# Key and value loads of a cached-attention decode block: from SyncE's queue to GpSimd's, with a signal from ScalarE to TensorE

## The chip, the cores and the metric

The kernel runs on one core of one Trainium2 chip. The metric is device time in microseconds (us), the median of several runs. A core has TensorE (PE), VectorE (DVE), ScalarE (ACT), GpSimd (POOL) and SyncE (SP); transfers from the chip's memory run on the core's 16 DMA engines, and any of SyncE, ScalarE and GpSimd can issue them from its instruction stream.

## What is computed

One decode step of a transformer block for 2 sequences: attention with a cached K and V of 8192 positions and 32 heads of 128 elements, then a gated feed-forward, all in float32.

```
h  = x + attention(layernorm(x), k_cache, v_cache, wq, wo)      # q = x wq; softmax(q k / sqrt(128)) v; times wo
h2 = h + (silu(n w_gate) * (n w_up)) w_down,  n = layernorm(h)
x [2,1,512]   k_cache, v_cache [2,32,8192,128]   wq [512,4096]   wo [4096,512]
w_gate, w_up [512,1792]   w_down [1792,512]
```

K and V together are 537 MB, nearly all that is read.

## The kernel before

The work is cut into 32 units. A unit `i` is two heads of one sequence: one head lies on partitions 0 to 63, the other on 64 to 127, and each partition holds 128 positions of 128 elements, 64 KB. So one K load and one V load are 8.39 MB each. There are two buffers for K (`kslot`, unit `i` uses number `i % 2`) and one for V (`vslot`). The buffers are used again at the two ends: `vslot` first holds wq and last w_down, and the two K buffers hold wo, and the gate and up weights, once their K is used up.

The loads stand in one list, `loads`, in this order: wq; K 0 in four parts; then K 1, V 0, K 2, V 1, and so on to K 31, V 30; then wo in two parts; V 31 in four parts; the gate and up weights in four parts; w_down in five. Before, SyncE issues them all in that order (L578 to L581), and ahead of a load into a used buffer it waits until the buffer's last reader is done (`after`, `freed`). For K `i` that is VectorE's last reduction over K `i-2`; for V `i` it is TensorE's last value matmul of unit `i-1`; for V 0 the last matmul of the query projection; for wo it is K 30, for V 31 it is V 30, for the gate and up weights K 31, for w_down V 31.

A round of the loop at L403, unit `i`, puts on VectorE: multiply the first half of K `i` with the query (L412); the maximum over partitions for unit `i-1` (`biggest`, L365); reduce the first half (L421); multiply the second half; the reciprocal of the softmax sum of unit `i-1` (`recip`, L391); reduce the second half; the maximum of the scores (L429). Unit 0 is done in four quarters. ScalarE has per round, for unit `i-1`: copy the negated maximum (L372), two exponentials (L378), then `rdiag` (L393), which needs the reciprocal of L391, then the copy of the value product (`osb`, L398) and of the transposed result (L400). ScalarE works through its instructions in order.

TensorE's rounds are a counted loop (`pe_rounds`, L342): the maximum's transpose (L314), its broadcast (L316, L317), the softmax sums (L319), then a wait for V, then the 64 value matmuls (`pe_values`, L324), then four small matmuls per unit (L337) that scale and transpose. The wait for V is on semaphore `s_v`, which each load raises by 16 and which TensorE lowers by 16 each round. The last unit's values are taken in four parts behind the loop, as the parts of V 31 land (L473).

GpSimd sets up constants (L207 to L216, L263), does one small power operation in each of the two layer norms (L236), and nothing else. `g.steps` holds each engine's instructions in the order in which the program adds them; `wait` leaves a wait out where the engine has already waited for as much.

Of the kernel before, what the change touches and what calls it, by code (L numbers as in the profile page):

```python
# [9 lines left out]
P = 128  # L10
# [3 lines left out]
class Program:  # L14
# [16 lines left out]
    def wait(self, engine, *points):  # L31
        for s, value in points:
            if self.known[engine].get(s, 0) < value:
                self.known[engine][s] = value
                self.steps[engine].append(lambda e, s=s, v=value: e.wait_ge(s, v))

    def do(self, engine, fn, sem=None, by=1):

        if sem is None:
            self.steps[engine].append(fn)  # L40
            return None
        self.count[sem] += by
        self.steps[engine].append(lambda e: fn(e).then_inc(sem, by))
        return sem, self.count[sem]
# [8 lines left out]
def decode_block(nc, x, k_cache, v_cache, wq, wo, w_gate, w_up, w_down, out):  # L53
# [24 lines left out]
    def sbuf(name, *shape, align=32):  # L78
        return nc.alloc_sbuf_tensor(name, list(shape), F32, align_bytes=align).ap()
# [7 lines left out]
    vslot = sbuf("vslot", P, SLOT, align=512)  # L87
# [38 lines left out]
    g = Program(nc)  # L126
    wait, do = g.wait, g.do
# [2 lines left out]
    s_dve, s_act, s_pe, s_pool = (g.sem(n) for n in ("dve", "act", "pe", "pool"))  # L130
    s_dve_pe, s_act_pe, s_v = (g.sem(n) for n in ("dve_pe", "act_pe", "v"))
    s_k = [g.sem(f"k{n}") for n in range(2)]

    def alone(name):
        return g.sem(name)
# [3 lines left out]
    landed = {}  # L139
    freed = {}  # L140
    loads = []
# [5 lines left out]
    def load_kv(kind, i, parts=1):  # L147
        cache, t = (k_cache, kslot[i % 2]) if kind == "k" else (v_cache, vslot)
        n = SLOT // parts
        for c in range(parts):  # L150
            sem = alone(f"{kind}{i}_{c}") if parts > 1 else s_k[i % 2] if kind == "k" else s_v
            loads.append(((kind, i), c, t[:, c * n : (c + 1) * n], k_src(cache, i)[:, c * n : (c + 1) * n], sem))

    loads.append((("wq", 0), 0, vslot, wq.rearrange("(p c) m -> p (c m)", p=P), s_v))
    load_kv("k", 0, 4)
    for i in range(1, U):
        load_kv("k", i)
# [21 lines left out]
    for e, (c, n) in enumerate(WF):  # L179
        src, c0 = (w_gate, c) if c < DC else (w_up, c - DC)  # L180
# [18 lines left out]
    after = {("v", 0): ("wq", 0), ("wo", 0): ("k", U - 2), ("wf", 0): ("k", U - 1), ("wd", 0): ("v", U - 1)}  # L199
# [28 lines left out]
    def layernorm(src, ready):  # L228
        wait("vector", *ready)
        p = do("vector", lambda e: e.bn_stats(stats, src), s_dve)  # L230
        wait("vector", p)
        p = do("vector", lambda e: e.bn_aggr(mv, stats), s_dve)
        wait("vector", p)
        p = do("vector", lambda e: e.tensor_scalar(ve, mv[:, 1:2], EPS, None, op0=OP.add), s_dve)
        wait("gpsimd", p)
        p = do("gpsimd", lambda e: e.tensor_tensor(rstd, ve, mhalf, op=OP.pow), s_pool)  # L236
        wait("vector", p)
        p = do(
            "vector",
            lambda e: e.tensor_scalar(y, src, mv[:, 0:1], rstd, op0=OP.subtract, op1=OP.mult),  # L240
            s_dve,
        )
        normed = p
        wait("tensor", p, ident_done)
        for c in range(DC):
            p = do(
                "tensor",
                lambda e, c=c: e.transpose(yt[:, c, :], y.rearrange("b (p c) -> b c p", c=DC)[:, c, :], ident[:B, :B]),
                s_pe if c == DC - 1 else None,
            )  # L250
        return normed, p

    _, p = layernorm(xs, [(x_in, 16)])
# [14 lines left out]
    p = do("vector", lambda e: e.tensor_copy(xT, yt), s_dve)  # L268
# [10 lines left out]
    for n, (m, b) in enumerate((m, b) for m in range(0, MQ, 4) for b in range(B)):  # L279
# [3 lines left out]
        for c in range(DC):  # L283
            for k in range(2):
                p = do(
                    "tensor",
                    lambda e, ps=ps, c=c, k=k, m=m, b=b: e.matmul(  # L287
                        ps[HALF[k]],
                        xb[:, c * B + b, :],
                        wqv[:, c, k, m : m + 4, :],  # L290
                        start=(c == 0),
                        stop=(c == DC - 1),
                    ),
# [40 lines left out]
    def pe_outputs(e):  # L334
        e.wait_ge(s_act_pe, 2)
        for a in range(W):
            inst = e.matmul(  # L337
                ot_ps, osb[:, a * DH : (a + 1) * DH], rdiag[:, a::W], start=(a == 0), stop=(a == W - 1)
            )
        inst.then_inc(s_pe, 1)  # L340

    def pe_rounds(e):  # L342
        e.sem_inc(s_v, -16)
        with nc.Fori(0, U - 1, engines=[PE], head_slot={PE: 0}):
            pe_scores(e)
            e.wait_ge(s_v, 16)
            pe_values(e, 0, NW)
            pe_outputs(e)
            e.sem_inc(s_dve_pe, -2)
            e.sem_inc(s_act_pe, -2)  # L350
            e.sem_inc(s_v, -16)
        pe_scores(e)

    g.steps["tensor"].append(pe_rounds)
# [6 lines left out]
    def biggest(i):  # L361
        wait("vector", at(i, MROW))
        do(
            "vector",
            lambda e: e.tensor_reduce(gm, mrow.rearrange("p (k r) -> p k r", k=2), axis=AX.X, op=OP.max),  # L365
            s_dve_pe,
        )
# [21 lines left out]
    def recip(i):  # L389
        wait("vector", at(i, DEN))  # L390
        p = do("vector", lambda e: e.reciprocal(r, den), s_dve)  # L391
        wait("scalar", p)
        do("scalar", lambda e: e.activation(rdiag, diag, AF.Copy, scale=r))  # L393
# [9 lines left out]
    for i in range(U):  # L403
        m, b = divmod(i, B)
        parts = 4 if i == 0 else 2
        n = NJ // parts
        wait("vector", q_done[m // 4 * B + b])
        for c in range(parts):
            wait("vector", landed[("k", i), c if i == 0 else 0])
            kt = k_view(i, c * n, n)  # L410
            qb = qsb[:, b, m, :][:, None, :].to_broadcast([P, n, DH])
            mult = do("vector", lambda e, kt=kt, qb=qb: e.tensor_tensor(kt, kt, qb, op=OP.mult), s_dve)  # L412
            if i and c == 0:
                biggest(i - 1)
                softmax(i - 1)
            if i and c == 1:
                recip(i - 1)
            wait("vector", mult)
            p = do(
                "vector",  # L420
                lambda e, kt=kt, s=scores[i % 2][:, c * n : (c + 1) * n]: e.tensor_reduce(s, kt, axis=AX.X, op=OP.add),  # L421
                s_dve,
            )
        freed["k", i] = p
        if i:
            oT_done[i - 1] = outputs(i - 1)
            freed["v", i - 1] = at(i - 1, PV)
        wait("vector", p)
        do("vector", lambda e, s=scores[i % 2]: e.tensor_reduce(m1, s, axis=AX.X, op=OP.max), s_dve_pe)  # L429
    biggest(U - 1)  # L430
    softmax(U - 1)
    do("scalar", lambda e: e.activation(warm, mhalf[:1, :], AF.Sigmoid))
# [10 lines left out]
    for c in range(4):  # L443
        for q in range(4):
            p = do(
                "tensor",
                lambda e, c=c, q=q: e.matmul(
                    oq_ps[32 * q : 32 * q + 32, c], ident[:, c::4], oT[:, q:QH:4, :], start=True, stop=True
                ),
                s_pe if c == 3 and q == 3 else None,  # L450
            )
    wait("scalar", p)
    p = do("scalar", lambda e: e.activation(oq, oq_ps, AF.Copy), s_act)
# [3 lines left out]
    for n, (o, w) in enumerate(pairs):  # L457
        t = n % 4
        p = do(
            "tensor",  # L460
            lambda e, n=n, t=t, o=o, w=w: e.matmul(
                wide[0][32 * t : 32 * t + B, :], o, w, start=(n < 4), stop=(n >= len(pairs) - 4)
            ),
            s_pe if n == len(pairs) - 1 else None,
        )
    wait("scalar", p)
    p = do("scalar", lambda e: e.activation(osb, wide[0], AF.Copy), s_act)
# [56 lines left out]
    p = project_f(0, gate)  # L524

    wait("tensor", h1_done)
    for t in range(4):
# [8 lines left out]
    p = do("scalar", lambda e: e.activation(sg, gate, AF.Sigmoid), s_act)  # L536
    wait("vector", p)
    sg_done = do("vector", lambda e: e.tensor_mul(sg, gate, sg), s_dve)
    p = project_f(DC, up)
# [4 lines left out]
    p = do(  # L544
        "vector",
        lambda e: e.tensor_mul(
            gu.rearrange("p (c j) -> p j c", c=FB),
            up.rearrange("p (j c) -> p j c", c=FB),
            sg.rearrange("p (j c) -> p j c", c=FB),
        ),  # L550
        s_dve,
    )
    gT = rest[:, D + 2 * FQ : D + 3 * FQ]
    wait("vector", p)
    p = do("vector", lambda e: e.transpose(gT, gu), s_dve)
    wait("tensor", p)
    for c in range(FB):
# [3 lines left out]
        for t in range(4):  # L561
            p = do(
                "tensor",
                lambda e, c=c, t=t: e.matmul(  # L564
                    f_ps[32 * t : 32 * t + 32, :],
                    gT[:, c * 32 : (c + 1) * 32],
                    vslot[:, c * D + t * P : c * D + (t + 1) * P],
                    start=False,
                    stop=(c == FB - 1),
                ),  # L570
# [4 lines left out]
    res_done = do("vector", lambda e: e.tensor_copy(res, f_ps), s_dve)  # L575


    for item, e_, dst, src, sem in loads:  # L578
        if item in after:
            wait("sync", freed[after[item]])  # L580
        do("sync", lambda e, dst=dst, src=src: e.dma_start(dst, src), sem, 16)  # L581
    stored = []
    for b, engine in enumerate(("sync", "scalar")):
        wait(engine, res_done)
# [52 lines left out]
```

## Time and profile before

| | |
|---|---|
| time, median of 3 runs | 1310.69 us (1310.65 to 1310.78) |
| span of the profiled execution | 1309.4 us |
| VectorE busy | 1131.0 us (86%) |
| TensorE matmuls busy | 432.7 us (33%) |
| ScalarE busy | 80.3 us (6%) |
| read from memory | 564.66 MB, 431 GB/s over the span |
| K loads 1 to 31, issue to landing (median) | 42.4 us |
| V loads 0 to 30, issue to landing (median) | 29.3 us |

The span is the time from the first to the last instruction of the one execution that was profiled; the times of the runs also hold what lies around it. In the profile PE is TensorE's matmuls, PEld its weight loads, and "SPq" the stream in which SyncE issues transfers. A line of the timeline gives start, duration, engine, line of the code, operation, the tiles written and read, their shapes and the count; in brackets stands the idle time of the engine before it and what ended that. A row of the windows gives the stretch, the busy time of PE, PEld, DVE, ACT and POOL with their counts, TensorE's granted clock, the share of time in which the DMA engines were busy, and GB/s. A row of the waits gives total, times, longest. A row of the queues gives packets, MB, and the share of the 16 engines' span.

### The profile page before, as it was taken

What the parts mean: (1) busy time and instruction counts of PE and PEld (TensorE: products, weight loads), DVE (VectorE), ACT (ScalarE), POOL (GpSimd) and SP (SyncE); (2) the same over time, 40 slices, a digit from 0 to 9 for tenths busy, and PEclk for the clock granted to TensorE, in tenths of its full rate; (3) what the DMA queues carried; (4) which work ended last, traced back from release to release, by engine and by line L of the source; (5) the groups of instructions that cost most, each with busy time, mean ns of one, the idle gap of its engine ahead of it and who ended that gap; (6) DMA issues with size and microseconds to landing.
All of it is one profiled execution on the core that took longest, in us unless ns stands there. A gap on an engine that the chain in (4) does not pass through costs nothing.

```text
span 1309.4 us, 6768 instructions
## 1 busy us (share of the span) xinstructions
PE 432.7 (33%) x2980; PEld 135.3 (10%) x2980; DVE 1131.0 (86%) x248; ACT 80.3 (6%) x271; POOL 2.9 (0%) x13
## 2 busy tenths in 40 slices
PE   3633223333213333312333321333332133332175
PEld 1210001011001011100101100101110010110022
DVE  1999888889888889988888988888998888898841
ACT  0100000000000000000000000000000000000010
POOL 0000000000000000000000000000000000000000
PEclk9865566666556666656666655666655666665589
DMA  9999999999999999999999999999999999999998
GB/s 401 435 442 426 438 435 434 439 426 442 422 442 422 444 432 436 438 426 442 422 442 422 444 434 434 439 426 440 424 441 424 442 436 432 440 424 442 414 429 368
DMA packets 12990, 564.79 MB, mean 431 GB/s; under 512 B 1322, under 2 KB 1330, under 8 KB 2484
## 3 DMA queue, kind: packets, MB, share of 16 engines
q1 hardware_dynamic: 12968, 564.67, 99.7%
q8 instruction: 5, 0.08, 0.0%
q14 instruction: 5, 0.04, 0.0%
q10 hardware_dynamic: 12, 0.01, 0.0%
HBM read 564.66 MB, written 0.00 MB: 431 GB/s over the span
## 4 chain that ended last, share of the span: by engine, by line
DMA 75%; PE 24%; issue 0%; SPq 0%; DVE 0%
DMA vslot<-in_A_v_cache_dram 72%; PE opart L324 22%; PE wide L287 2%; DMA vslot<-in_A_wq_dram 2%; DMA vslot<-in_B_w_down_dram 2%; SPq L581 0%; PE bank L564 0%; DVE kslot L575 0%
## 5 line engine op out<-in xcount | busy, mean ns | idle before, releaser
L412 DVE TENSOR_TENSOR kslot<-kslot,qsb 128x8192 f32<-128x8192 f32 (+1 forms) x66 | 555.9, 8422 | 127.4 <-DMA kslot<-in_A_k_cache_dram 104.4
L421 DVE TENSOR_REDUCE s<-kslot 128x64 f32<-128x8192 f32 (+1 forms) x66 | 555.5, 8417 | 0.1
L324 PE MATMUL opart<-vslot,pz 128*8 128x512 f32 x2048 | 293.7, 736 | 253.7 <-DMA vslot<-in_A_v_cache_dram 253.7
L316 PE MATMUL bank<-gm,nscale 1*64 1x1 f32 x64 | 11.8, 251 | 361.7 <-DVE gm L365 361.7
L324 PEld LDWEIGHTS opart<-vslot,pz 128*8 128x8 f32 x2048 | 57.4, 103 | 463.0 <-DMA vslot<-in_A_v_cache_dram 257.9
L314 PE MATMUL bank<-ident,m 128*1 128x128 f32 x64 | 18.7, 395 | 163.3 <-DVE m L429 163.3
L316 PEld LDWEIGHTS bank<-gm,nscale 1*64 1x64 f32 x64 | 9.1, 199 | 377.7 <-DVE gm L365 377.7
L337 PE MATMUL bank<-rdiag,osb 128*128 128x2 f32 x256 | 33.7, 254 | 23.7 <-ACT osb L398 23.7
L393 ACT ACTIVATE rdiag<-diag,r 128x8 f32<-128x8 f32 x32 | 9.6, 301 | 484.6 <-DVE r L391 484.6
L372 ACT ACTIVATE nb<-bank 128x1 f32<-128x1 f32 x32 | 5.5, 171 | 550.2 <-PE bank L317 550.2
L337 PEld LDWEIGHTS bank<-rdiag,osb 128*128 128x128 f32 x256 | 31.0, 191 | 53.4 <-ACT osb L398 53.4
L287 PE MATMUL wide<-vslot,osb 128*64 128x512 f32 x128 | 29.6, 626 | 17.5 <-DMA vslot<-in_A_wq_dram 17.5
L319 PE MATMUL bank<-rs,sides 128*128 128x1 f32 x64 | 18.8, 363 | 41.5 <-ACT pz L378 41.5
L378 ACT ACTIVATE pz<-s,nb 64x128 f32<-64x128 f32 x64 | 25.5, 399 | 1.4
L398 ACT ACTIVATE osb<-opart 128x512 f32<-128x512 f32 x32 | 19.1, 597 | 76.6 <-PE opart L324 76.6
L230 DVE BATCH_NORM_STATS2 ln_stats<-attn 2x6 f32<-2x512 f32 x1 | 0.7, 687 | 25.2 <-PE attn L489 25.2
L319 PEld LDWEIGHTS bank<-rs,sides 128*128 128x128 f32 x64 | 16.1, 313 | 44.2 <-ACT pz L378 44.2
L314 PEld LDWEIGHTS bank<-ident,m 128*1 128x1 f32 x64 | 2.7, 81 | 166.9 <-DVE m L429 166.9
L287 PEld LDWEIGHTS wide<-vslot,osb 128*64 128x64 f32 x128 | 10.3, 145 | 36.0 <-issue 36.0
L378 ACT ACTIVATION_READ_ACCUMULATOR pz<-s,nb 64x1 f32 x64 | 11.8, 185 | 0.0
L317 PE MATMUL bank<-gm,nscale 1*64 1x1 f32 x64 | 11.8, 251 | 0.0
L429 DVE TENSOR_REDUCE m<-s 128x1 f32<-128x128 f32 x32 | 9.2, 286 | 1.1
(60 smaller groups left out, 84.2 us busy)
## 6 DMA issues: line engine op xcount, KB each, us to landing
kslot<-in_A_k_cache_dram SPq DMA_DIRECT2D x4, 2048.0 KB, 32.9
vslot<-in_A_v_cache_dram SPq DMA_DIRECT2D x4, 2048.0 KB, 22.2
kslot<-in_A_wo_dram SPq DMA_DIRECT2D x1, 7168.0 KB, 40.3
kslot<-in_B_w_gate_dram SPq DMA_DIRECT2D x1, 3584.0 KB, 32.1
vslot<-in_B_w_down_dram SPq DMA_DIRECT2D x2, 1024.0 KB, 18.5
kslot<-in_B_w_up_dram SPq DMA_DIRECT2D x1, 1792.0 KB, 36.0
kslot<-in_B_w_up_dram SPq DMA_DIRECT2D x2, 896.0 KB, 38.5
kslot<-in_A_wo_dram SPq DMA_DIRECT2D x1, 1024.0 KB, 42.4
```

The lines of the kernel that those rows point to most:

```text
L287: lambda e, ps=ps, c=c, k=k, m=m, b=b: e.matmul(ps[HALF[k]], xb[:, c * B + b, :], wqv[:, c, k, m : m + 4, :], start=(c == 0), stop=(c == D ...
L314: e.matmul(mrow, m1, ident, start=True, stop=True).then_inc(s_pe, 1)
L316: e.matmul(nb_ps[HALF[0]], nscale, gm[:, 0:1], start=True, stop=True)
L317: e.matmul(nb_ps[HALF[1]], nscale, gm[:, 1:2], start=True, stop=True).then_inc(s_pe, 1)
L319: e.matmul(den, sides.rearrange("p w a -> p (w a)"), rs, start=True, stop=True).then_inc(s_pe, 1)
L324: inst = e.matmul(opart[32 * t : 32 * t + 2 * W, :], pz[:, w, :], vslot[:, w * W * DH : (w + 1) * W * DH], start=(w < 4), stop=(w >= NW - 4),)
L337: inst = e.matmul(ot_ps, osb[:, a * DH : (a + 1) * DH], rdiag[:, a::W], start=(a == 0), stop=(a == W - 1))
L378: lambda e, k=k, h=h: e.activation(pz[h, :, k * W : (k + 1) * W], s[h].rearrange("p (w a) -> p w a", a=W), AF.Exp, bias=nb[h], scale=SCALE ...
L393: do("scalar", lambda e: e.activation(rdiag, diag, AF.Copy, scale=r))
L398: do("scalar", lambda e: e.activation(osb, opart, AF.Copy), s_act_pe)
L412: mult = do("vector", lambda e, kt=kt, qb=qb: e.tensor_tensor(kt, kt, qb, op=OP.mult), s_dve)
L421: lambda e, kt=kt, s=scores[i % 2][:, c * n : (c + 1) * n]: e.tensor_reduce(s, kt, axis=AX.X, op=OP.add),
```

## The change

K loads 1 to 31 and V loads 0 to 30 are issued by GpSimd, in their old order among themselves and with the old waits. SyncE keeps wq, the four parts of K 0, wo, the four parts of V 31, and the feed-forward weights. GpSimd's part stands in its program behind the constants and ahead of the second layer norm. wq gets a semaphore of its own in place of `s_v`.

TensorE no longer waits for V in its loop. ScalarE waits for V of unit `i-1` and then raises a new semaphore `v_here` by one; TensorE waits for that and lowers it by one. On ScalarE the wait and the raise stand right behind `recip(i-1)`, that is behind `rdiag`, and ahead of `osb`.

```diff
+    s_here = g.sem("v_here")
...
-    loads.append((("wq", 0), 0, vslot, wq.rearrange("(p c) m -> p (c m)", p=P), s_v))
+    loads.append((("wq", 0), 0, vslot, wq.rearrange("(p c) m -> p (c m)", p=P), alone("wq")))
...
     def pe_rounds(e):
-        e.sem_inc(s_v, -16)
         with nc.Fori(0, U - 1, engines=[PE], head_slot={PE: 0}):
             pe_scores(e)
-            e.wait_ge(s_v, 16)
+            e.wait_ge(s_here, 1)
             pe_values(e, 0, NW)
             pe_outputs(e)
             e.sem_inc(s_dve_pe, -2)
             e.sem_inc(s_act_pe, -2)
-            e.sem_inc(s_v, -16)
+            e.sem_inc(s_here, -1)
         pe_scores(e)
...
             if i and c == 1:
                 recip(i - 1)
+                wait("scalar", landed[("v", i - 1), 0])
+                g.steps["scalar"].append(lambda e: e.sem_inc(s_here, 1))
...
+    def issue(engine, these):
+        for item, e_, dst, src, sem in these:
+            if item in after:
+                wait(engine, freed[after[item]])
+            do(engine, lambda e, dst=dst, src=src: e.dma_start(dst, src), sem, 16)
+
+    by_pool = [x for x in loads if x[0][0] in "kv" and x[4] in (s_v, *s_k)]
+    issue("gpsimd", by_pool)
     biggest(U - 1)
...
-    for item, e_, dst, src, sem in loads:
-        if item in after:
-            wait("sync", freed[after[item]])
-        do("sync", lambda e, dst=dst, src=src: e.dma_start(dst, src), sem, 16)
+    issue("sync", [x for x in loads if x not in by_pool])
```

## The prediction

> **What bounds the kernel now.** I read the table of DMA queues first, then the windows, the waits, the chain of work, and last the timeline of one round, of the start and of the end.
>
> ```profile
> span 1309.4 us, 6768 instructions
> ...
> GB/s 401 435 442 426 438 435 434 439 426 442 422 442 422 444 432 436 438 426 442 422 442 422 444 434 434 439 426 440 424 441 424 442 436 432 440 424 442 414 429 368
> ...
> q1 hardware_dynamic: 12968, 564.67, 99.7%
> ...
> q10 hardware_dynamic: 12, 0.01, 0.0%
> ...
> 0.00:22.70 22.70, 0.64 (x4) 0.55 (x4) 2.94 (x10) 1.28 (x1) 2.31 (x12) 1.00 0.93 389
> ...
> 101.30:565.00 463.70, 140.31 (x960) 43.47 (x960) 420.93 (x84) 26.67 (x96) 0.00 (x0) 0.62 1.00 434
> ...
> 565.17:603.77 38.60, 12.41 (x80) 3.71 (x80) 35.08 (x8) 2.22 (x8) 0.00 (x0) 0.59 1.00 435
> ```
>
> One queue, SyncE's, moves 564.67 MB and keeps the 16 DMA engines occupied for 99.7% of the span. The last three columns of a window are clock, DMA share and GB/s: share 1.00 and 434 GB/s for hundreds of microseconds. The kernel is bound by its transfers, and any time in which the DMA engines have no work is lost for good. One load of K or V is 8.39 MB, so 19.3 us at 434 GB/s; a round moves two of them, 38.6 us, which is the length of the third window. That window is one round, from VectorE's start on one K block to its start on the next:
>
> ```profile
> 565.17 8.69 DVE L412 TENSOR_TENSOR kslot<-kslot,qsb 128x8192 f32<-128x8192 f32 x1 [3.56 <-DMA kslot<-in_A_k_cache_dram]
> ...
> 575.54 0.18 ACT L378 ACTIVATION_READ_ACCUMULATOR pz<-s,nb 64x1 f32 x1
> ...
> 575.77 0.59 PE L319 MATMUL bank<-rs,sides 128*128 128x1 f32 x2 [1.30 <-ACT pz L378]
> ...
> 582.57 8.67 DVE L412 TENSOR_TENSOR kslot<-kslot,qsb 128x8192 f32<-128x8192 f32 x1
> ...
> 584.47 9.81 PE L324 MATMUL opart<-vslot,pz 128*8 128x512 f32 x64 [8.11 <-DMA vslot<-in_A_v_cache_dram]
> ...
> 591.17 0.15 DVE L391 RECIPROCAL r<-bank 128x1 f32<-128x1 f32 x1
> ...
> 591.36 0.30 ACT L393 ACTIVATE rdiag<-diag,r 128x8 f32<-128x8 f32 x1 [15.63 <-DVE r L391]
> ...
> 594.35 0.33 SPq L581 DMA_DIRECT2D vslot<-in_A_v_cache_dram  x1
> 594.35 0.60 ACT L398 ACTIVATE osb<-opart 128x512 f32<-128x512 f32 x1 [2.70 <-PE opart L324]
> ...
> 599.99 0.33 SPq L581 DMA_DIRECT2D kslot<-in_A_k_cache_dram  x1
> 600.00 0.29 DVE L429 TENSOR_REDUCE m<-s 128x1 f32<-128x128 f32 x1
> ...
> 603.77 8.69 DVE L412 TENSOR_TENSOR kslot<-kslot,qsb 128x8192 f32<-128x8192 f32 x1 [3.49 <-DMA kslot<-in_A_k_cache_dram]
> ...
> 623.15 9.24 PE L324 MATMUL opart<-vslot,pz 128*8 128x512 f32 x64 [8.19 <-DMA vslot<-in_A_v_cache_dram]
> ...
> 632.47 0.33 SPq L581 DMA_DIRECT2D vslot<-in_A_v_cache_dram  x1
> ```
>
> Count from 565.17. TensorE's 64 value matmuls (L324) start at 19.3, when V lands, and the next V load is ordered at 29.2. The next K lands at 38.6, so the V load is ordered 9.4 us before the queue runs out. That lead keeps the DMA engines full. VectorE is done at 35.1 and waits 3.5 us for K: it is no bound by itself. The reciprocal (26.0) and ScalarE's rdiag, which ends at 26.49, come while the value matmuls already run. That order is what the change touches.
>
> **The change, part by part.** *ScalarE's signal.* Before, TensorE itself waits for V. After, ScalarE waits for V and then raises v_here, and this stands in ScalarE's program behind recip, that is behind rdiag. So the value matmuls can't start before 26.5 + 0.1 (a hop between engines; L319 starts some 0.05 us after the last L378 ends) = 26.6, though V lands at 19.3. What is queued behind the wait on ScalarE is osb (L398), which needs the value matmuls anyway, then the next softmax, far off. On TensorE it is the value matmuls and all that follows. The matmuls took 9.81 and 9.24 us, and the V load was ordered 9.88 and 9.32 us after their start: 9.6 in the mean. So the next V load is ordered at 26.6 + 9.6 = 36.2, not 29.2, and only 2.4 us ahead of the next K's landing.
>
> What must fit into these 2.4 us? The nearest row is the first load, which had the queue to itself:
>
> ```profile
> 0.73 22.01 DMA vslot<-in_A_wq_dram
> 22.88 29.66 PE wide L287 x128
> ...
> 3.61 0.54 POOL L236 TENSOR_TENSOR ln_rstd<-ln_ve,mhalf 2x1 f32<-2x1 f32 x1 [2.01 <-DVE ln_ve L234]
> ...
> 5.05 0.21 POOL L263 MEMSET hT<- 128x128 f32 x1
> ```
>
> 22.01 us for a transfer of 19.3 us leaves 2.7 us: the window to 22.70 has 389 GB/s where 434 would be full, so 2.35 us passed before data flowed (1.5 after the issue began), and the other 1.2 us lie between the last data and the waiting engine's start. *GpSimd's own price* is in no row, for no DMA is issued by GpSimd before. Its bounds: 0 (as SyncE), and four software passes of the 0.54 us that GpSimd takes for a 2x1 operation, 2.2 us. A gain over SyncE is excluded where the GpSimd program has to compute what is issued. I take one pass, 0.5 us, nearest to that row.
>
> The Trainium skill, "DMA: Bandwidth & Descriptors", section Specifications, gives some 1 us to the first byte from GpSimd and 0.6 us from SyncE; by its difference of 0.4 us the sum would be an estimated 1.4 us lower.
>
> *The sum of a round.* From VectorE's start on K block i: V load ordered at 36.2, overhead 2.7 + 0.5, then V and the K behind it, 38.6: VectorE starts on K block i+2 at 78.0. With full DMA engines it would be 77.2. That is 0.8 us lost in two rounds, 0.4 in each, over some 28 rounds **11.2 us**. (With 0 extra 0.15 a round, 4 us; with 2.2 extra 1.25 a round, 35 us.)
>
> *The start.* GpSimd is free at 5.05 + 0.21 = 5.3, so K load 1 flows from about 7.3, beside wq instead of behind wq and K 0. How two queues share the engines is in no row (q10 moved 0.01 MB): the bounds are nothing and everything, and I take half each, the middle, for want of a row that leans to either.
>
> The Trainium skill, "DMA: Bandwidth & Descriptors", section Queues, rings and completion order, says that each DMA engine goes round the queues packet by packet; with equal packets that is half each, and the sum would be the same.
>
> ```profile
> 29.16 4.43 DVE L412 TENSOR_TENSOR kslot<-kslot,qsb 128x4096 f32<-128x4096 f32 x1 [23.07 <-ACT qsb L298]
> ...
> 64.64 8.68 DVE L412 TENSOR_TENSOR kslot<-kslot,qsb 128x8192 f32<-128x8192 f32 x1
> ...
> 1183.73 8.69 DVE L412 TENSOR_TENSOR kslot<-kslot,qsb 128x8192 f32<-128x8192 f32 x1 [3.53 <-DMA kslot<-in_A_k_cache_dram]
> ...
> 1218.55 0.99 SPq L581 DMA_DIRECT2D kslot<-in_A_wo_dram  x2
> ...
> 1250.65 1.76 SPq L581 DMA_DIRECT2D vslot<-in_A_v_cache_dram  x4
> ...
> kslot<-in_A_wo_dram SPq DMA_DIRECT2D x1, 7168.0 KB, 40.3
> ...
> kslot<-in_A_wo_dram SPq DMA_DIRECT2D x1, 1024.0 KB, 42.4
> ```
>
> At 7.3 wq has had 4.95 of its 19.3 us; the other 14.35 take 28.7 at half rate, to 36.0. K 1 then has 4.95 left, which it shares with the first quarter of K 0 (4.8): that ends at 45.7 and lands at 46.9. VectorE's four quarters took from 29.16 to 64.64, 35.5 us; now they end at 82.4, and only then does VectorE begin on K 1. Value matmuls of block 0 end 36.2 later, and V load 1 flows from 82.4 + 36.2 + 2.0 = 120.6. Before, with full engines, it was the sixth load: 2.35 + 5 x 19.3 = 98.9. Lost: **21.7 us** (some 8 of it sooner: V 0 waits for the 29.66 us of projection behind the late wq). VectorE's slack of 3.5 us a round doesn't give it back, since from here the DMA engines are the bound again.
>
> *The end.* SyncE no longer stands behind V 30: it issues wo when K 30 is free, 34.8 us after 1183.73. GpSimd orders V 30 at 36.2. K 31 ends at 37.4; wo (7168 + 1024 KB, as much as one load) flows from 36.3, V 30 from 38.2. Both share 38.6 us of work and end at 76.0, V 30 last. It lands at 77.2, its matmuls end at 86.8, and only then go the four parts of V 31, flowing from 88.3; the gate and up weights stand behind them on SyncE. The engines idle from 76.0 to 88.3, **12.3 us**. Before, V 31 was ordered at 66.9 with wo still ahead of it in the queue.
>
> *At no cost:* SyncE's issue time (0.33 us a load, beside transfers); wq's own semaphore; the extra ScalarE and TensorE counts, beside VectorE's 35 us. If SyncE's queue holds nothing else, nobody waits for it in the rounds.
>
> The sum: 21.7 + 11.2 + 12.3 = 45.2 us. The profiled span is 1309.4 and the median 1310.69, so 1.3 us lie around it: 1309.4 + 45.2 + 1.3 = **1356 us**.
>
> **The rivals.** *Another share.* If SyncE's queue goes first, wq and K 0 keep their times; V 1 flows at 64.6 + 36.2 + 2.0 = 102.8, 4 us late; the end still costs 12.3, since V 30 comes last: 1338. If GpSimd's goes first, wq ends at 41, VectorE ends K 0 at about 84, 23.3 us lost; but V 30 lands by 59 and its matmuls end at 74.8, so the end costs 0.3: 1345. Nothing in before speaks for either.
> *The signal isn't held* by the reciprocal (ScalarE gets past its wait sooner): the rounds cost nothing, the start 8.7 (V 0 behind the projection), the end 12.3: 1332. The code speaks against it.
> *Slower transfers.* If loads from GpSimd's queue ran at 422 GB/s, the lowest of the inner slices of the page's GB/s line (401, 414 and 368 stand at the ends), a round would take 39.8, 1.16 more, in place of the 0.4; with 30 rounds 35 us: 1380.
> *VectorE holds GpSimd up.* If GpSimd's issue had to wait for a multiplication of 8.69 us begun at 38.6, each order would slip to 47.3: 6 us a round, 167 in all, with the start and the end 201: 1512. It decides only where the order misses the gap between 35.1 and 38.6, and 36.2 lies in it.
> The Trainium skill, "SBUF — State Buffer", section Who interferes with whom, speaks against the change here: GpSimd can't write its descriptors while VectorE copies in certain modes; it excepts the multiplication and reduction of these rounds, so by it this rival falls; no run so far shows it.
> *Not slower: faster transfers.* A queue of its own could move more than 434 GB/s. Two rounds would be 36.2 + 3.2 plus two loads. To make good the 34 us of start and end, a round must fall to 37.4, a load to 17.7 us: 474 GB/s is the point. At 500 GB/s a round takes 36.5, and the time is 1285. Against it: share 1.00 at 434 GB/s, so the engines, not their orders, are full.
>
> **How the numbers follow.** Forecast 0.58; another share 0.18; not held 0.04; slower transfers 0.12; held up by VectorE 0.03; not slower 0.05, of it 0.03 faster and 0.02 within 0.2%, which is about what a measurement of this kernel can tell from no change. The range: low is SyncE first with no cost in the rounds, 16.3 us, 1327; high the forecast with GpSimd's upper price, 21.7 + 35 + 12.3, 1380, which also holds the slower transfers. Slower has 0.95.
>
> **What would show it.** Right: value matmuls starting just behind rdiag, released by ScalarE; K landings 39.0 apart; wq landing near 37; V 1 ordered near 118; a gap of some 12 us in the transfers before V 31. Wrong: value matmuls still 19.3 behind VectorE's start; wq landing at 22.9; two queues with unequal bytes where both have work; windows inside the rounds far from 434 GB/s; a V order from GpSimd that takes over 2 us to flow.

## The result, and the profile after

| | before | after |
|---|---|---|
| time, median of 5 runs | 1310.69 us (1310.45 to 1310.89) | 1353.93 us (1349.94 to 1357.60) |
| ratio | | 1.0333, 95% interval 1.0322 to 1.0344 |
| profiled execution: time, span | span 1309.4 us | 1353.78 us, span 1352.4 us |

Slower by 43.2 us, 3.3%; the spans differ by 43.0 us. The runs also lie further apart, 7.7 us in place of 0.4.

The lines of the page of the kernel after that answer to those of before:

```profile
span 1352.4 us, 6798 instructions
...
GB/s 407 338 415 273 432 430 434 434 434 432 432 407 434 432 434 432 405 403 403 434 434 426 428 419 434 433 434 428 409 435 405 432 432 407 434 415 434 439 410 366
...
q0 software_dynamic: 8928, 520.10, 89.6%
q1 hardware_dynamic: 4040, 44.57, 7.8%
...
L325 PE MATMUL opart<-vslot,pz 128*8 128x512 f32 x2048 | 296.0, 741 | 469.4 <-ACTq L419 467.0
```

520.10 MB have gone over to a queue of their own, q0. The two queues' shares add to 97.4% where SyncE's alone had 99.7%, and the GB/s line has two deep slices near the start (338 and 273) and shallow ones (403 to 419) all along. The value matmuls (L325, L324 before) wait for ScalarE's raise of `v_here` (L419), no longer for V.

To see where the 43.0 us come from, cut the span at two marks that both kernels have: VectorE's start on K 3 and on K 31. The windows of the profile between them, before and then after (with three more that are used below):

```profile
139.96:1222.35 1082.39, 331.54 (x2240) 101.91 (x2240) 982.17 (x196) 62.24 (x224) 0.00 (x0) 0.61 1.00 434
```

```profile
60.00:70.00 10.00, 7.59 (x36) 2.50 (x32) 9.93 (x4) 1.79 (x3) 0.54 (x1) 1.00 0.38 129
107.00:121.00 14.00, 11.29 (x74) 2.92 (x74) 13.96 (x5) 1.07 (x3) 1.05 (x2) 0.74 0.22 75
160.08:1263.92 1103.84, 324.01 (x2240) 101.99 (x2240) 982.19 (x197) 62.26 (x224) 28.95 (x55) 0.61 0.99 425
...
1290.00:1302.00 12.00, 10.98 (x74) 2.92 (x74) 9.07 (x4) 1.07 (x3) 0.00 (x0) 0.78 1.00 417
```

| part | before | after | more | forecast |
|---|---|---|---|---|
| start, to K 3 | 139.96 | 160.08 | 20.1 | 21.7 |
| 28 rounds, K 3 to K 31 | 1082.39 | 1103.84 | 21.5 | 11.2 |
| end, from K 31 | 87.05 | 88.48 | 1.4 | 12.3 |
| sum | 1309.4 | 1352.4 | 43.0 | 45.2 |

The total came within 2.2 us of the forecast, but two of its three terms are wrong, by 10 us each, in opposite directions.

**The start**, in the timeline of after:

```profile
5.29 0.70 POOL L437 DMA_DIRECT2D kslot<-in_A_k_cache_dram  x1
...
37.17 30.41 PE L288 MATMUL wide<-vslot,osb 128*64 128x512 f32 x128 [31.66 <-DMA vslot<-in_A_wq_dram]
...
46.83 4.43 DVE L412 TENSOR_TENSOR kslot<-kslot,qsb 128x4096 f32<-128x4096 f32 x1 [40.61 <-DMA kslot<-in_A_k_cache_dram]
...
67.90 0.54 POOL L437 DMA_DIRECT2D vslot<-in_A_v_cache_dram  x1 [61.91 <-PE wide L288]
...
82.30 8.68 DVE L412 TENSOR_TENSOR kslot<-kslot,qsb 128x8192 f32<-128x8192 f32 x1
...
118.81 0.53 POOL L437 DMA_DIRECT2D vslot<-in_A_v_cache_dram  x1 [35.92 <-PE opart L325]
```

K 1 is ordered at 5.29, beside wq; wq lands at 37.17 where it landed at 22.88. Everything behind it is late by as much: V 0 waits for the projection until 67.90, VectorE comes to K 1 at 82.30, and V 1 is ordered at 118.81. The windows 60 to 70 (129 GB/s) and 107 to 121 (75 GB/s) are the two deep slices: the DMA engines wait for these two orders.

**A round** of after, and one order ahead of it:

```profile
550.36 0.53 POOL L437 DMA_DIRECT2D vslot<-in_A_v_cache_dram  x1 [40.31 <-PE opart L325]
...
553.39 8.69 DVE L412 TENSOR_TENSOR kslot<-kslot,qsb 128x8192 f32<-128x8192 f32 x1 [3.76 <-DMA kslot<-in_A_k_cache_dram]
...
579.58 0.30 ACT L393 ACTIVATE rdiag<-diag,r 128x8 f32<-128x8 f32 x1 [15.63 <-DVE r L391]
579.65 9.89 PE L325 MATMUL opart<-vslot,pz 128*8 128x512 f32 x64 [15.06 <-ACTq L419]
589.88 0.53 POOL L437 DMA_DIRECT2D vslot<-in_A_v_cache_dram  x1 [38.47 <-PE opart L325]
...
594.63 8.69 DVE L412 TENSOR_TENSOR kslot<-kslot,qsb 128x8192 f32<-128x8192 f32 x1 [6.12 <-DMA kslot<-in_A_k_cache_dram]
```

The value matmuls start 26.26 us behind VectorE's start on K (579.65 - 553.39), where they started at 19.3, and V is ordered at 36.49; the mean over the rounds is 35.9. This round is 41.24 long; the mean is 1103.84 / 28 = 39.42, before 38.66.

**The end:**

```profile
1260.03 1.74 SPq L437 DMA_DIRECT2D kslot<-in_A_wo_dram  x2
1260.70 0.53 POOL L437 DMA_DIRECT2D vslot<-in_A_v_cache_dram  x1 [37.72 <-PE opart L325]
1263.92 8.69 DVE L412 TENSOR_TENSOR kslot<-kslot,qsb 128x8192 f32<-128x8192 f32 x1 [3.59 <-DMA kslot<-in_A_k_cache_dram]
...
1290.18 9.62 PE L325 MATMUL opart<-vslot,pz 128*8 128x512 f32 x64 [15.06 <-ACTq L419]
...
1299.87 1.76 SPq L437 DMA_DIRECT2D vslot<-in_A_v_cache_dram  x4
```

wo and V 30 are ordered together. V 30's matmuls start at 1290.18, 26.26 behind VectorE's start: that is the signal again, and V 30 was there by then. V 31 is ordered at 1299.87, while wo still flows, and the window 1290 to 1302 has 417 GB/s: no gap.

### The profile page after: what moved, and what is told of

Its sections match the earlier page's. It is cut to its first block, busy times and chain, and to the rows that moved or that the text cites. A ratio compares the mean times of both kernels' runs of the same rounds, so it can differ in the third digit from the quotient of the medians.

```text
span 1352.4 us, 6798 instructions
## 1 busy us (share of the span) xinstructions
PE 426.9 (32%) x2980; PEld 136.0 (10%) x2980; DVE 1131.0 (84%) x248; ACT 80.4 (6%) x271; POOL 35.7 (3%) x75
## 3 DMA queue, kind: packets, MB, share of 16 engines
q0 software_dynamic: 8928, 520.10, 89.6%
## 4 chain that ended last, share of the span: by engine, by line
DMA 54%; DVE 34%; PE 11%; POOL 1%; issue 0%; SPq 0%; ACT 0%; DVEq 0%
DMA kslot<-in_A_k_cache_dram 50%; DVE kslot L412 22%; DVE s L423 11%; PE opart L325 11%; DMA vslot<-in_A_v_cache_dram 2%; DMA vslot<-in_B_w_down_dram 2%; POOL vslot L437 1%; DVE gm L365 0%; SPq L437 0%; DVE r L391 0%; PE bank L575 0%; ACT rdiag L393 0%; DVE kslot L586 0%; DVEq L35 0%; DVE m L431 0%
## 5 line engine op out<-in xcount | busy, mean ns | idle before, releaser
L423 DVE TENSOR_REDUCE s<-kslot 128x64 f32<-128x8192 f32 (+1 forms) x66 | 555.5, 8417 | 0.1
L325 PE MATMUL opart<-vslot,pz 128*8 128x512 f32 x2048 | 296.0, 741 | 469.4 <-ACTq L419 467.0
L325 PEld LDWEIGHTS opart<-vslot,pz 128*8 128x8 f32 x2048 | 57.7, 104 | 680.6 <-ACTq L419 469.6
L437 POOL DMA_DIRECT2D vslot<-in_A_v_cache_dram x31 | 16.4, 530 | 1208.9 <-PE opart L325 1147.0
L320 PEld LDWEIGHTS bank<-rs,sides 128*128 128x128 f32 x64 | 16.1, 313 | 44.2 <-ACT pz L378 44.2
L315 PE MATMUL bank<-ident,m 128*1 128x128 f32 x64 | 12.4, 275 | 14.9 <-DVE m L431 14.9
L437 POOL DMA_DIRECT2D kslot<-in_A_k_cache_dram x31 | 16.6, 537 | 14.2 <-DVE s L423 13.9
## 6 DMA issues: line engine op xcount, KB each, us to landing
vslot<-in_A_v_cache_dram SPq DMA_DIRECT2D x4, 2048.0 KB, 16.1
```

What stands on the lines that cost most here:

```text
L315: e.matmul(mrow, m1, ident, start=True, stop=True).then_inc(s_pe, 1)
L320: e.matmul(den, sides.rearrange("p w a -> p (w a)"), rs, start=True, stop=True).then_inc(s_pe, 1)
L325: inst = e.matmul(opart[32 * t : 32 * t + 2 * W, :], pz[:, w, :], vslot[:, w * W * DH : (w + 1) * W * DH], start=(w < 4), stop=(w >= NW - 4),)
L437: do(engine, lambda e, dst=dst, src=src: e.dma_start(dst, src), sem, 16)
```

## The experiments

Three questions: what does each part of the change cost (1 to 3, 6, 8); how do two queues share the engines (4, 5, 7); why do the rounds lose 0.77 us and not 0.4 (7, 9 to 11). Each edit is against the kernel after. A ratio is against the kernel before, with its 95% interval.

**1. The signal alone**, all loads on SyncE.

```diff
-    issue("gpsimd", by_pool)
...
-    issue("sync", [x for x in loads if x not in by_pool])
+    issue("sync", loads)
```

> The loads stay on SyncE; only ScalarE's signal is new. Theory A (late orders: the signal behind the reciprocal puts V's order some 36 us after VectorE's start, and the transfers run dry): the rounds lose 0.3 to 0.8 us each, 8 to 22 us in all, V 1 flows some 3.4 us late, the end costs nothing: 1320 to 1336 us, V orders 36 us behind VectorE's start. Theory B (GpSimd's queue itself is what costs: dearer orders or slower transfers): with SyncE's queue the late order fits, 1311 to 1317 us.

Measured: 1328.70 us (1325.00 to 1334.50), ratio 1.0151 (1.0122 to 1.0181). Its timeline:

```profile
572.57 8.69 DVE L412 TENSOR_TENSOR kslot<-kslot,qsb 128x8192 f32<-128x8192 f32 x1 [3.56 <-DMA kslot<-in_A_k_cache_dram]
...
598.82 8.58 PE L325 MATMUL opart<-vslot,pz 128*8 128x512 f32 x64 [15.06 <-ACTq L419]
607.47 0.33 SPq L437 DMA_DIRECT2D vslot<-in_A_v_cache_dram  x1
...
612.54 8.69 DVE L412 TENSOR_TENSOR kslot<-kslot,qsb 128x8192 f32<-128x8192 f32 x1 [4.86 <-DMA kslot<-in_A_k_cache_dram]
```

The value matmuls are held to the same 26.25 us (598.82 - 572.57) without GpSimd's queue. The signal's place alone costs 18 us. With SyncE's queue the rounds are 39.04 us long.

**2. The signal early, the queue as changed**: the wait and the raise go ahead of `rdiag`.

```diff
             if i and c == 0:
                 biggest(i - 1)
                 softmax(i - 1)
+                wait("scalar", landed[("v", i - 1), 0])
+                g.steps["scalar"].append(lambda e: e.sem_inc(s_here, 1))
             if i and c == 1:
                 recip(i - 1)
-                wait("scalar", landed[("v", i - 1), 0])
-                g.steps["scalar"].append(lambda e: e.sem_inc(s_here, 1))
```

> GpSimd's queue as in the changed kernel; ScalarE waits for V and signals ahead of rdiag, not behind it. Theory A: value matmuls start again as V lands, 19.3 us behind VectorE's start, V is ordered 9 us ahead of the queue's end and the rounds cost nothing; left are the start, where V 0 waits for the late projection (8.7 us), and 1 us at the end: 1319 to 1322 us. Theory B: the rounds still lose the 0.8 us each of the changed kernel: 1338 to 1345 us.

Measured: 1319.93 us (1319.43 to 1320.37), ratio 1.0069 (1.0052 to 1.0085). One order of its timeline, and its window from 101.30:

```profile
592.63 9.38 PE L325 MATMUL opart<-vslot,pz 128*8 128x512 f32 x64 [8.18 <-ACTq L417]
602.35 0.53 POOL L437 DMA_DIRECT2D vslot<-in_A_v_cache_dram  x1 [32.12 <-PE opart L325]
...
611.87 8.69 DVE L412 TENSOR_TENSOR kslot<-kslot,qsb 128x8192 f32<-128x8192 f32 x1 [3.51 <-DMA kslot<-in_A_k_cache_dram]
```

```profile
101.30:1183.73 1082.43, 336.42 (x2266) 104.44 (x2258) 993.08 (x199) 62.80 (x226) 30.11 (x57) 0.61 1.00 434
```

With the order 9.5 us ahead of VectorE's next start, GpSimd's queue runs at 434 GB/s as SyncE's did. wq still lands at 37.24, and V 0 is ordered at 67.09: VectorE starts on K 31 8.6 us later than before, and the end takes 0.9 us more. So the 9.2 us that stay in the median are nearly all the start's.

**3. K 1 back on SyncE**, the rest as changed (K 1 has a semaphore of its own, so `by_pool` leaves it out).

```diff
-            sem = alone(f"{kind}{i}_{c}") if parts > 1 else s_k[i % 2] if kind == "k" else s_v
+            sem = alone(f"{kind}{i}_{c}") if parts > 1 or (kind, i) == ("k", 1) else s_k[i % 2] if kind == "k" else s_v
```

> K 1 alone goes back to SyncE behind K 0. Theory A with the start's loss as K 1's doing: wq lands near 23 instead of 37 us, VectorE begins on K 1 at 65 to 68 instead of 82.3, V 1 is ordered near 104 instead of 118.8, 12 to 18 us less than the changed kernel: 1335 to 1342 us. If the start's loss is GpSimd's slow first orders and not K 1's share, the time stays at 1350 or more.

Measured: 1338.05 us (1334.02 to 1349.36), ratio 1.0236 (1.0192 to 1.0281). wq lands at 22.92 and VectorE starts on K 3 at 144.34, 15.7 us sooner than after; the median is 15.9 lower. That one load beside wq costs 16 us here. (The four runs lie far apart, so the start on K 3 in the trace is the surer of the two figures.)

**4. K 1 in rows of 8 KB** in place of 64 KB, still from GpSimd and beside wq.

```diff
+        if (kind, i) == ("k", 1):
+            n = SLOT // 8
+            for c in range(8):
+                loads.append(((kind, i), 7 - c, t[:, c * n : (c + 1) * n], k_src(cache, i)[:, c * n : (c + 1) * n], s_k[1]))
+            return
```

> K 1 goes in 8 loads with rows of 8 KB instead of one with rows of 64 KB, still from GpSimd. If the engines go round the queues packet by packet, wq (64 KB packets) gets 8 parts of 9: it lands near 25 us, VectorE begins on K 1 near 67, the start loses 6 us instead of 21.7: 1336 to 1341 us. If two queues get equal bytes whatever their packets, wq lands at 37 us as before and the time is 1354 us.

Measured: 1339.69 us (1336.96 to 1343.70), ratio 1.0224 (1.0200 to 1.0248). The timeline of this kernel, where L293 is the projection:

```profile
24.71 8.78 PE L293 MATMUL wide<-vslot,osb 128*64 128x512 f32 x30 [19.59 <-DMA vslot<-in_A_wq_dram]
```

The same bytes from the same queue, and wq lands at 24.71, not 37.17. The two queues take turns by the packet, and a packet is one row of a load: from 8 to 23 us the trace has 80 packets of 64 KB of wq and 80 packets of 8 KB of K 1. With 8 parts of 9, the 14.35 us that wq still needs at 7.3 take 16.1, to 23.4, and 1.2 more is 24.6.

**5. wo in rows of 56 KB** in place of 8 KB. The rows of wo then stand in another order, so this kernel's output is another one; it moves as many bytes.

```diff
-        wo_t[:, : QH * D].rearrange("p (h m) -> p h m", m=4 * D),
-        wo[: QH * DH].rearrange("(h p c) m -> p h (c m)", p=P, c=4),
+        wo_t[:, : QH * D],
+        wo[: QH * DH].rearrange("(p c) m -> p (c m)", p=P),
```

> As the changed kernel, but the first 28 heads of wo are read in rows of 56 KB, not 8 KB (another order of wo's rows, so the output is another one). Packet by packet, V 30 (64 KB packets) then no longer has 8 parts of 9 against wo but about half: it lands some 12 us later than in the changed kernel, V 31 is ordered that much later and the transfers run dry before it, the 12 us of the forecast: 1362 to 1368 us. If V 30 went first for another reason (its queue, its order), nothing changes: 1350 to 1358 us.

Measured: 1362.76 us (1359.04 to 1368.47), ratio 1.0402 (1.0369 to 1.0434). Its timeline at the end:

```profile
1259.01 0.53 POOL L437 DMA_DIRECT2D vslot<-in_A_v_cache_dram  x1 [37.53 <-PE opart L325]
1266.13 8.69 DVE L412 TENSOR_TENSOR kslot<-kslot,qsb 128x8192 f32<-128x8192 f32 x1 [8.21 <-DMA kslot<-in_A_k_cache_dram]
...
1300.59 9.06 PE L325 MATMUL opart<-vslot,pz 128*8 128x512 f32 x64 [23.27 <-ACTq L419]
1309.72 1.88 SPq L437 DMA_DIRECT2D vslot<-in_A_v_cache_dram  x4
```

Now V 30 does take 41.6 us from order to matmul, and V 31 is ordered 43.6 us behind VectorE's start on K 31 where it was 35.95. From 1302 to 1310 the DMA engines move 2 GB/s, a gap of 8 us. This is the end that the prediction described, if not its whole 12.3 us; the kernel has it only with long rows.

**6. The signal early and K 1 on SyncE** (the edits of 2 and 3 together).

> The signal ahead of rdiag and K 1 back on SyncE: GpSimd issues K 2 to 31 and V 0 to 30. Theory A (late orders and K 1's share are the whole cost, the queue costs nothing): as before the change, 1309.5 to 1312 us. Theory B (GpSimd's queue costs something by itself): 1316 us or more.

Measured: 1310.45 us (1310.24 to 1311.62, 10 runs), ratio 0.9999 (0.9990 to 1.0009). 61 of the loads still go through GpSimd. Where its orders come early, the queue itself costs nothing.

**7. Every K and V load as two loads with rows of 32 KB.** Against the theory of that moment, that the rounds' added delay is one packet long.

```diff
+        if parts == 1:
+            n = SLOT // 2
+            for c in range(2):
+                sem = s_k[i % 2] if kind == "k" else s_v
+                loads.append(((kind, i), 1 - c, t[:, c * n : (c + 1) * n], k_src(cache, i)[:, c * n : (c + 1) * n], sem))
+            return
```

> As the changed kernel, but each K and V load from GpSimd goes as two loads with rows of 32 KB. In the changed kernel V landed up to 2.75 us later than both the previous K's landing and V's order allow, which is near the 2.4 us in which one engine moves a 64 KB packet. If that delay goes by the packet, it falls to 1.2 us at most, the rounds lose some 0.4 us each, not 0.8: 1340 to 1348 us. If it doesn't, 1352 to 1358 us.

Measured: 1353.84 us (1352.74 to 1357.33), ratio 1.0334 (1.0316 to 1.0351): no different from after, its rounds 39.51. That theory fell. The run gives a third point for the sharing, in its timeline (L294 is the projection):

```profile
30.09 3.42 PE L294 MATMUL wide<-vslot,osb 128*64 128x512 f32 x8 [24.80 <-DMA vslot<-in_A_wq_dram]
```

With 64 KB of wq to 32 KB of K 1 in each turn, wq has two parts of three: the 14.35 us that it needs from 7.3 on take 21.5, to 28.8, and 1.2 more is 30.0.

**8. All on SyncE, the signal early** (the edits of 1 and 2 together).

> All loads on SyncE, ScalarE's signal ahead of rdiag. Theory A: the signal by itself costs nothing where it doesn't hold the value matmuls back: 1310 to 1311.5 us. If a hop through ScalarE costs time by itself: 1314 us or more.

Measured: 1310.41 us (1310.16 to 1311.56, 10 runs), ratio 0.9999 (0.9989 to 1.0008). ScalarE's signal is free where it isn't held.

**9. The reciprocal and the signal behind the second reduction**, loads as changed: V's orders come about 8 us later still.

```diff
             if i and c == 1:
                 recip(i - 1)
                 wait("scalar", landed[("v", i - 1), 0])
                 g.steps["scalar"].append(lambda e: e.sem_inc(s_here, 1))
```

These lines stand behind the reduction of L423 in place of ahead of it.

> As the changed kernel, but VectorE takes the reciprocal, and ScalarE the signal, behind the second reduction: 8.7 us later still. Then every second V order comes with the transfers dry. Order to landing on idle engines was 21.9 us in the changed kernel. If that price holds, two rounds take the order's offset, 35.0 + 9.6 + 0.3 = 44.9, and 21.9 + 19.3: 86.1 us, a round 43.1, and with a start lost of 29 and an end of 8 us the time is near 1472 us. If the unexplained part of the changed kernel's rounds (0.4 us each) stands on top wherever an order is late, a round takes 43.4 or more, 1482 us.

Measured: 1463.44 us (2 runs, 1462.48 and 1464.40), ratio 1.1162 (1.1130 to 1.1194), rounds 42.81. Expected were 1472 us and 43.1: V's orders came 44.1 us behind VectorE's start in the mean, not 44.9.

```profile
467.15 8.69 DVE L412 TENSOR_TENSOR kslot<-kslot,qsb 128x8192 f32<-128x8192 f32 x1 [5.92 <-DMA kslot<-in_A_k_cache_dram]
470.31 0.53 POOL L437 DMA_DIRECT2D vslot<-in_A_v_cache_dram  x1 [43.53 <-PE opart L325]
```

Here V is ordered at 470.31, in the midst of VectorE's multiplication (467.15 to 475.84). By the trace's packets the 16 engines begin on it between 471.55 and 472.46, so VectorE does not hold GpSimd's issue up. With the engines empty a V order takes 22.1 us to land (median), and its first packet starts 1.24 us behind the order.

**10. The same, all on SyncE** (the edits of 9 and 1 together).

> The same with all loads on SyncE. What GpSimd adds to each late order is then read off: its orders came 0.26 us behind the matmuls' end and took 0.53 us to issue, SyncE's 0.05 and 0.33. If that is all, a round is 0.1 to 0.3 us shorter than with GpSimd, 42.8 to 43.0, and the start costs 11 us less or more, about 1450 us. If GpSimd's queue adds more where engines are dry, the rounds differ by 0.5 us or more.

Measured: 1442.90 us (2 runs, 1442.89 and 1442.92), ratio 1.1005 (1.0973 to 1.1037), rounds 42.69, where 1450 us and 42.8 to 43.0 were expected. With the engines empty, as at every second order here, V takes 21.9 us from order to landing (median), and the first packet starts 0.97 us behind the order. So GpSimd's own price is some 0.3 us an order, and a round is 0.12 longer with it.

**11. VectorE takes K in quarters, the reciprocal behind the third multiplication**: the signal is still held behind the reciprocal, which comes sooner.

```diff
-        parts = 4 if i == 0 else 2
+        parts = 4
...
-            if i and c == 1:
+            if i and c == 2:
```

> As the changed kernel, with ScalarE's signal still behind the reciprocal, but VectorE works each K in quarters and takes the reciprocal behind the third multiplication, 22.2 us after its start instead of 26.0. V's order then comes some 32 us after VectorE's start and 6 us ahead of the next K's landing. If it is that lead alone which decides (no loss was seen above 4.5 us), the rounds lose nothing: a round 38.7 us, the start 4 us less than in the changed kernel, 1327 to 1333 us. If the signal's place behind the reciprocal or GpSimd's queue costs by itself, rounds stay above 39.2 us and the time above 1345 us.

Measured: 1328.58 us (1327.99 to 1329.53), ratio 1.0139 (1.0122 to 1.0156).

```profile
574.13 0.53 POOL L437 DMA_DIRECT2D vslot<-in_A_v_cache_dram  x1 [34.15 <-PE opart L325]
...
581.12 4.43 DVE L412 TENSOR_TENSOR kslot<-kslot,qsb 128x4096 f32<-128x4096 f32 x1 [3.03 <-DMA kslot<-in_A_k_cache_dram]
```

V is ordered 7.0 us ahead of VectorE's next start (6.0 to 8.1 over the rounds), and the rounds are back at 38.7, before 38.66. So what the rounds cost goes by how far ahead V is ordered, not by the signal's standing behind the reciprocal as such. The queue costs nothing in them where the order is this early.

**The trace's packets.** Why do the rounds of after lose twice what was forecast? The trace has a record of each packet: start, duration, size. A 64 KB packet takes 2.418 us, and on an engine each begins within 0.02 us of its predecessor's end, so 16 chains, one for each DMA engine, can be told apart in the records. Two things can be added up on each chain between VectorE's starts on K 3 and on K 31: time between packets, and time by which a packet took longer than 2.418. Means of the 16 engines, in us:

```
                                   between packets   longer packets
before                                  0.13              0.20
after                                  10.91             10.99
1  signal alone, SyncE                  1.74              8.55
2  signal early, GpSimd                 0.12              0.11
11 reciprocal sooner, GpSimd            0.11              0.26
```

The 21.9 us of after are the 21.5 that its rounds are longer. Half is stops, half is packets that follow late orders: 328 packets of after took over 2.5 us, 2.91 in the mean, and 277 of them began within 6 us of a V order. In kernels 2 and 11, whose V orders come 6 us or more ahead, there is neither.

How a stop looks can be seen in the DMA view of after from 548 to 558 us, around the V order of 550.36. Its GB/s line has 40 slices of 0.25 us, each with the packets that start in it, so that 262 is one packet of 64 KB and 2097 are eight:

```profile
GB/s 2097 0 0 0 0 0 0 0 0 0 262 0 0 0 1311 1835 524 262 0 0 0 0 0 0 0 0 1049 2097 1049 0 0 0 0 0 0 262 1573 1835 262 262
```

Packets start every 2.4 us. After those of 548.0, 16 should start about 550.4: one does (the 262 in the eleventh slice), the last packet of K on one engine. The 15 others are done with K between 550.2 and 550.7 and stand still until 551.6 to 552.4 (5 + 7 + 2 + 1 packets). VectorE gets K when the one engine is done, 553.08, and starts at 553.39. So the order that stands 3.0 us ahead of VectorE's start came when 15 of 16 engines were at their end. The one engine, too, stands still, from 553.08 to 554.59. It has 16 packets of V and K before it, and nobody takes any of them over: 14 of 2.418 us and two longer ones (3.17, the first, and 2.73) end at 554.59 + 39.7 = 594.3, and VectorE's next start is 594.63. The round is 41.24 long, 2.6 more than 38.66, the engines' mean loss around that order 2.1, the worst engine's 2.53.

The other rounds read alike. Where the order comes over 3.8 us ahead of VectorE's start the mean loss of the engines is 0.2 us or less, but for one round (4.74 ahead, 1.04) in which again the last engine was a packet behind; what was expected of kernel 11 overlooked that round. From 2.0 to 3.1 it is 0.2 to 2.2, and in between one order of six loses 1.4, the others under 0.2. At one lead the queue does count: over the orders that stood 2.2 to 3.2 us ahead, the engines stood still for 0.78 us in the mean with GpSimd's queue (after, 12 orders) and for 0.14 with SyncE's (kernel 1, 7 orders). What this doesn't settle is why the first packets after a late order take longer, and why a single engine that was ordered on 2.7 us before its end stands still all the same. Kernel 7 says only that shorter packets don't cure it.

## Why the prediction was right in the sum, and where it was wrong

**Bound by its transfers: right.** Kernels 2 and 6 fill the engines at 434 GB/s through GpSimd, and are as long as before but for the start of kernel 2 (and 0.9 us at its end).

**The signal's place: right, in its mechanism.** "The value matmuls can't start before 26.6": they started at 26.26 (ScalarE's raise passes as rdiag starts, not as it ends), released by ScalarE, and V was ordered at 35.9, forecast 36.2. Kernel 1 shows that this alone costs 18 us, kernel 8 that the signal costs nothing where it isn't held.

**The start, 21.7 forecast, 20.1 measured: right, step by step.** wq 37.2 (37.2), first quarter of K 0 at 46.83 (46.9), K 1 at 82.30 (82.4), V 1 ordered at 118.81 (118.6). Kernel 3 takes K 1 from beside wq and wins 16 us. Half each was right for wq and K 1 because both have rows of 64 KB. For K 1 and the first quarter of K 0 it was luck: K 0's quarters have rows of 16 KB, K 1 went ahead and landed at 43.1, and the quarter came when it did because the two had nearly the same amount left, so that the last of them ends at the same time however they share. The DMA view of after, 6 to 34 us and then 1264 to 1280 us:

```profile
q1 hardware_dynamic: 96, 6.29, 51.9%
q0 software_dynamic: 86, 5.64, 46.4%
...
q0 software_dynamic: 96, 6.29, 90.7%
q1 hardware_dynamic: 144, 1.18, 17.4%
```

**The end, 12.3 forecast, 1.4 measured: wrong at the step "both share 38.6 us of work and end at 76.0, V 30 last".** Half each was carried over to wo and V 30, but the turn is a packet, not a number of bytes: the second pair of rows above has 6.29 MB of V 30 (64 KB packets) to 1.18 MB of wo (8 KB packets). In its first 2 us V 30's packets are only beginning; from 1266 to 1280 it is 80 packets of each, 5.24 MB to 0.66. V 30 landed 27.4 us after its order, not 41, in time for the signal, and V 31 was ordered while wo still flowed. Kernel 5 gives wo rows of 56 KB and gets the end that was forecast in kind: V 30's matmuls 41.6 us behind its order, an end 8.4 us longer than before, 8.8 us more than after in the median. The Trainium skill, "DMA: Bandwidth & Descriptors", section Queues, rings and completion order, has the engines go round the queues packet by packet; the landings of wq agree, 37.2, 30.1 and 24.7 us beside K 1 in rows of 64, 32 and 8 KB. The prediction took from it only the case of equal packets, and did not ask how long wo's rows are.

**The rounds, 11.2 forecast, 21.5 measured: the mechanism right, the size half.** The failing step is "overhead 2.7 + 0.5, then V and the K behind it": it takes the 16 engines for one. By that sum an order 3.2 us ahead of VectorE's start is free (2.8 with the measured 22.05 us from order to landing), and the mean lead of after was 3.5; from the leads that came it gives some 0.3 us a round (0.1 with the 2.8). What came is 0.77. The engines end a packet apart, each stops by itself, VectorE waits for the last, and the packets after a late order are slow: 10.9 + 11.0 us on each engine. GpSimd's own price was sized at 0.5 us and is some 0.3 where the engines are empty, but with so little lead the queue makes far more of a difference: between packets 10.9 us with GpSimd, 1.7 with SyncE, and 9.4 us between the medians of kernels 3 and 1. That the 0.3 us decide how many engines stop would fit; no run shows it.

**The rivals.** *Another share* has the end for its kernel of truth: neither queue goes first, but long rows win. *The signal isn't held:* out, since TensorE is released behind rdiag; kernel 2 shows what it would be, 1319.93, which is the 1332 without the end's 12.3. *Slower transfers:* out as put, since kernel 2 runs at 434 GB/s; the 425 of after are half stops and half packets that take longer behind a late order. *VectorE holds GpSimd up:* out by kernel 9's orders in the midst of a multiplication. The Trainium skill, "SBUF — State Buffer", section Who interferes with whom, excepts the multiplication and the reduction of these rounds, and for the multiplication that kernel agrees, with 22.1 us from order to landing. *Faster transfers:* out, 434 GB/s again.

**The parts of the change.** In the medians the 43.2 us are 18.0 for the signal's place (kernel 1), 9.4 for GpSimd's queue under late orders (kernel 3 against 1) and 15.9 for K 1 beside wq (after against 3). They don't simply add: with the signal early, K 1 beside wq costs 9.5 (kernel 2 against 6) and the rest of the queue nothing (kernel 6).

So it was luck that 1356 came so near to 1353.93: an end too dear by 10.9 us made up for rounds too cheap by 10.3.

## What to carry to other kernels

A load that must follow closely on another has to be ordered well ahead of the moment when its data is first missed by any DMA engine: here 6 us or more ahead of VectorE's next start cost nothing (kernel 11), 2 to 3 us cost up to 2.2 us an order, and a signal put behind an unrelated wait of an engine that works in order took that lead away. Before a second queue is given work, ask what flows beside it: the share goes by packets, so beside rows as long as its own a load loses half, and beside 64 KB rows a load in 8 KB rows got one part in nine. And check a forecast by its terms, not by its total.

## What was not expected of the hardware

- The 16 DMA engines don't share a load's rest: one that is 2.4 us behind keeps its packets, and the landing waits for it (553.08 against 550.2 to 550.7 for the 15 others).
- A packet of 64 KB that follows a late order often took longer than 2.418 us: the 328 of after that took over 2.5 us took 2.91 in the mean, and with SyncE the 320 of kernel 1 took 2.78. Why is open.
- An order of 8.39 MB with the engines empty took 22.1 us to land from GpSimd and 21.9 from SyncE (medians of kernels 9 and 10): nearly no price for the software queue.
- The spread of the runs grows with small leads: 7.7 us in after (5 runs) and 9.5 in kernel 1 (4), against 1.7 before (19) and 1.4 in kernel 6 (10).
